# Building steps between a spectrum's products, other places for the first spectra, and nine kept blocks of weights loaded at once

## The chip, the cores and the metric

The kernel runs on one core of a Trainium2 chip. Its time is the device time of one execution in microseconds (us); lower is better. A core has TensorE (PE, matrix products into PSUM), VectorE (DVE), ScalarE (ACT), GpSimd (POOL) and SyncE (SP, which issues most of the DMAs). Each of them takes its instructions in program order, so the order in which the program emits work is the order in which each engine does it.

## What is computed

Two independent layers get the same length of sequence, 2048 rows, and their outputs stand side by side.

```
def _A_ref(x, mem0, Wq, Wk, Wv, Wo, seg_len):      # 64 segments of 32 rows, 8 memory rows
    for s in range(n_seg):
        h = concat([mem, xs])                      # q, k, v = h Wq, h Wk, h Wv; 32 heads of 128
        o = softmax(mask(q k^T)) v Wo
        mem = o[:, :M]
def _B_ref(u, A_re, A_im, B_re, B_im, C_re, C_im, log_dt, Dskip):
    K = einsum('dn,dnl,dn->dl', Cc, exp(logdA l), dB).real     # 1024 channels, 2048 taps
    y = irfft(rfft(pad(u)) * rfft(pad(K)))[:L] + u * Dskip     # a long convolution per channel
```

Layer A is a chain over 64 segments. Layer B is a convolution by Fourier transforms, which the kernel does as matrix products with tables of cosines and sines.

## The kernel before, in words

The program runs part B first (`part_b`) and then part A (`part_a`). What of part A doesn't depend on its chain is done inside part B, as side work.

Part B has these stages:

- Up to about 376 us it prepares parameters, makes tables of powers in sixteen steps (`for f in range(16)`), from which come the taps K, and beside that it transforms the input u. The transformed u goes to DRAM as `Ud`, the taps as `Kx` (copied out of a tile `KxT`, `put_values`) and, in other orders, as `Kp`.
- **The change lies from here on.** The forward matrices, which transform K, are built by `build(kc, ...)` for kc = 0 to 3: a generator of 14 steps. One step fills one PSUM bank on PE (two products of 256 columns that contract over 7 rows, L1187, or one of 512, L1191 and L1199) and empties it on ACT, with a sine (L1178) or, for the three amplitudes, a copy (L1200). Step 0 makes a basis, steps 1 to 5 the angles of half n = 0, steps 6 to 8 the amplitudes, steps 9 to 13 the angles of half n = 1. `make(kc, n)` runs the next n steps of one matrix. The banks come from a ring of three (`take`), which the tap products `kp` (`values`, L1064) use too, so a step waits until the bank used three turns before has been emptied. `weighted(kc, n)` multiplies the finished half by the amplitudes on DVE (L1209).
- `spectrum(b, n, outs)` is the product of half n of matrix b % 4 with the taps of quarter b // 4 of the channels: 20 products of 128x128 by 256 columns on PE (L1225), into two PSUM banks. Two pairs of such banks are in use (`halves`, from `ps_e`).
- The sixteen blocks `for b in range(16)` follow. `pointwise(b, s_)` multiplies the block's two spectra with u (`times_u`, two operations of L1381 per half), turns the parts (`rotate`, L1384 and L1385), and takes difference and sum (`odd` at L1471, `even` at L1472); POOL adds and subtracts those into the tile `Bt` (L1474, L1476, L1477). While it does this, the program emits the spectra of block b + 1. Each `times_u` needs its half of u, which `load_u(b)` (L1216, two loads of 512 KB into `uq`, named `wq` in the profile) fetches as soon as block b - 1 has been multiplied. From block 4 on, `inverses` does the inverse products of block b - 4 (L1513).
- `PLACES` says which of twelve slots holds which sum or difference of a quarter. Eight slots are in the tile `Bp`, which lies where `KxT` lay before; four (e2, o1, o3, s2) are in `Bq`, which lies where the tables lay. The profile calls both `Bt`.
- SP's queue in these blocks holds, in order of emission: `load_u(b + 1)`; small rearranged pieces of taps (`second`, `load_k`); pairs of skip rows (`load_pair`); two loads of 512 KB into `MI` for b < 4 (L1573), which are the inverse matrices; and then `next(resident)` as often as a table by b says: each loads 512 KB of part A's weights (L268), to be kept in SBUF. The first nine of these have memory of their own, the later ones take over places that part B has given up. Thirty have been issued after block 15 (table: 1 each for blocks 1 to 5, then 2, 2, 2, 3, 2, 3, 3, 2, 3, 3).
- Before the loop comes a hand-written order for the last table's operations (`absolute`, `minus`, `imaginary`, `cosine`, `real`, `values` and, for the copy into `KxT` at L1072, `table_ops["x"]`), matrices 0 and 1, and the spectra of blocks 0 and 1; matrix 2 is built at its end (`make(2, 14)`), matrix 3 in block 1, seven steps after each spectrum (`make(3, 7)`).

Part A then runs its 64 segments to the end, streaming a part of its weights from DRAM.

Of the kernel before, what the change touches and what calls it, by code (L numbers as in the profile page):

```python
# [687 lines left out]

COARSE = [(16, 32, 16), (544, 64, 8), (1088, 128, 8)]
FINE = [(-64, 8, 4), (-32, 4, 4), (-16, 1, 32), (16, 4, 4), (32, 8, 5)]  # L690
PLACES = ("e0 o0 e1 o1 e2 o2 e3 o3", "s0 s1 s2 s3 e0 e1 e2 e3", "o0 o1 o2 o3 s0 s2 e0 e2", "s1 s3 e1 e3 o0 o2 s0 e0")
TURNS = [(0, 1, 17), (20, 4, 4), (40, 8, 4)]
NC, NP, NN, NA = 32, 25, 24, 25
STEP, CENTER, ONE = 16, 192.0, 120
# [18 lines left out]
def part_b(ctx, tc, u, A_re, A_im, B_re, B_im, C_re, C_im, log_dt, Dskip, out_b, ahead, copies, residents, first_state):  # L713
# [6 lines left out]
    v, sc, gp, pe, sy = nc.vector, nc.scalar, nc.gpsimd, nc.tensor, nc.sync  # L720
# [57 lines left out]
    with tc.tile_pool(name="b_par", bufs=1) as par, tc.tile_pool(name="b_parh", bufs=2) as parh, \  # L778
# [190 lines left out]
        for word_ in PAR:  # L969
            word = word_.rstrip("/")  # L970
            nm, n_ = word[0], word[1:]
# [187 lines left out]
    G = {}  # L1159
# [46 lines left out]
    def weighted(kc, n_, amp):  # L1206
        a_ = amp.rearrange("p (j q) -> p j q", j=3)[:, :, 256 * n_:256 * n_ + 256]
        g_ = G[kc][:, n_, 2:5].rearrange("p j s h f -> p j s (h f)")
        v.tensor_tensor(out=g_, in0=g_, in1=a_.unsqueeze(2).to_broadcast([128, 3, 2, 256]), op=ALU.mult)  # L1209
# [5 lines left out]
        for n_ in range(2):  # L1215
            sy.dma_start(out=uq[n_], in_=Ud[b % 4, b // 4][:, 2 * n_:2 * n_ + 2].rearrange("p a c d -> p (a c d)"))  # L1216

    def spectrum(b, n_, outs, halves=(0, 1)):
        dq, kc = b // 4, b % 4
        KT = ks[dq // 2]  # L1220
        d = slice(DQ * (dq % 2), DQ * (dq % 2) + DQ)
        for half in halves:
            for cs in range(2):
                for j in range(5):
                    pe.matmul(outs[half][:, cs, :], lhsT=G[kc][:, n_, j, cs, half, :], rhs=KT[j][:, d], start=(j == 0), stop=(j == 4), skip_group_check=True)  # L1225

    T = {}
    pars = {0: par_t[0]}
# [13 lines left out]
    def cosines(r, h):  # L1242
        return T["n", r, h][:].bitcast(BF16)[:, 0:32 * NT]
# [39 lines left out]
    def cosine(r, h):  # L1283
        sc.activation(out=cosines(r, h), in_=T["n", r, h][:], func=ACT.Sin, scale=-TWO_PI, bias=hp[:])
# [5 lines left out]
    def imaginary(r, h):  # L1290
        products(r, h, "gi", windows(T.pop(("s", r, h))), T.pop(("w", r, h))[:])

    def real(r, h):
        c_ = cosines(r, h).rearrange("p (a b) -> p a b", a=32)
        products(r, h, "gr", c_, turned(c_))
# [30 lines left out]
    for f in range(16):  # L1326
# [7 lines left out]
        if f == 15:  # L1334
# [6 lines left out]
            amps = [wsl[0][:, 0:1536], wsl[3][:, 0:1536]] * 2  # L1341
# [28 lines left out]
    def make(kc, n):  # L1370
        for _ in range(n):
            next(made[kc])

    def halves(pool=ps_e):
        t_ = pool.tile([128, 2, 512], F32, name="pa", tag="pa")
        return [t_[:].rearrange("p h (c d) -> p h c d", c=2)]

    def times_u(s_, Z, n_, X=None):
        us = uq[n_].rearrange("p (a c d) -> p a c d", a=2, c=2)
        for i, t_ in ((1, Z), (0, s_[n_][0] if X is None else X)):  # L1380
            v.tensor_tensor(out=t_, in0=us[:, :, i, :].unsqueeze(2).to_broadcast([128, 2, 2, DQ]), in1=s_[n_][0], op=ALU.mult)  # L1381

    def rotate(Y, X, Z):
        v.tensor_tensor(out=Y[:, :, 0, :], in0=X[:, :, 0, :], in1=Z[:, :, 1, :], op=ALU.subtract)  # L1384
        v.tensor_tensor(out=Y[:, :, 1, :], in0=X[:, :, 1, :], in1=Z[:, :, 0, :], op=ALU.add)  # L1385
    now = [halves() for _ in range(2)]
# [2 lines left out]
    absolute(15, 0)  # L1389
    minus(15, 0)  # L1390
    make(0, 9)
    imaginary(15, 0)
    absolute(15, 1)
    minus(15, 1)
    imaginary(15, 1)
    make(0, 3)
    weighted(0, 0, amps[0])
    spectrum(0, 0, [now[0][0][:, half] for half in range(2)])
    make(0, 2)
    weighted(0, 1, amps[0])  # L1400
    spectrum(0, 1, [now[1][0][:, half] for half in range(2)])
    cosine(15, 0)
    cosine(15, 1)
    times_u(now, zs[0][:], 0, first[:, 0])
    real(15, 0)
    times_u(now, zs[1][:], 1, first[:, 1])
    load_u(1)
    real(15, 1)
    make(1, 9)
    for t in range(2):  # L1410
        values(15, t)
    make(1, 5)
    nxt_ = [halves()]
    weighted(1, 0, amps[1])
    spectrum(1, 0, [nxt_[0][0][:, half] for half in range(2)])
    for n_ in range(2):
        rotate(first[:, n_], first[:, n_], zs[n_][:])
    for t in range(2):
        table_ops["x"](15, t)
    weighted(1, 1, amps[1])  # L1420
    nxt_.append(halves())
    spectrum(1, 1, [nxt_[1][0][:, half] for half in range(2)])
    make(2, 14)
    for f_ in late:
        f_()
    for g in (pro, bg, mb, others):
# [27 lines left out]
    def spectra(dq, kc, odd_):  # L1454
        at = PLACES[dq].split()[2 * kc + odd_]
        return Bp[:, stay_.index(at)] if at in stay_ else Bq[:, ("e2", "o1", "o3", "s2").index(at)]

    def pointwise(b, s_):
        dq, kc = b // 4, b % 4
        if b:  # L1460
            times_u(s_, Zs[:, 0], 0)
            if b < 4:
                rotate(even, s_[0][0], Zs[:, 0])
            times_u(s_, Zs[:, 1], 1)
            if b > 3:
                rotate(even, s_[0][0], Zs[:, 0])
        yield
        if b:
            rotate(s_[1][0], s_[1][0], Zs[:, 1])
        Y = (even[:], s_[1][0]) if b else (first[:, 0], first[:, 1])  # L1470
        v.tensor_tensor(out=odd[:], in0=Y[0], in1=Y[1], op=ALU.subtract)  # L1471
        v.tensor_tensor(out=even[:], in0=Y[0], in1=Y[1], op=ALU.add)  # L1472
        for i, op in ((0, ALU.add), (1, ALU.subtract)):
            gp.tensor_tensor(out=spectra(dq, kc, 0)[:, i], in0=even[:, 0], in1=even[:, 1], op=op)  # L1474
        eng, to = v if b == 15 else gp, blocks(spectra(dq, kc, 1))
        eng.tensor_tensor(out=to[:, 0:4:3], in0=odd[:, 0], in1=odd[:, 1, ::-1], op=ALU.add)  # L1476
        eng.tensor_tensor(out=to[:, 2:0:-1], in0=odd[:, 0], in1=odd[:, 1, ::-1], op=ALU.subtract)  # L1477
# [52 lines left out]
    for b in range(16):  # L1530
        points = pointwise(b, now)
        next(points)
        if 0 < b < 15:
            load_u(b + 1)
        for _ in range(4 if b in (2, 3) else 0):
            second.pop(0)()
        if b == 2:
            ks.append([])
        if 2 <= b < 6:
            lo, hi = b - 2, min(b - 1, 3) if b < 5 else 5  # L1540
            ks[1].extend(load_k(1, k1[:, DH * lo:DH * hi], lo))
        if b >= 4:
            load_pair(b - 2, iv)
        if b == 3:
            v.tensor_scalar(out=ident[:], in0=ident[:], scalar1=float(PLEN / 2), scalar2=None, op0=ALU.mult)
            load_pair(0, iv)
            load_pair(1, iv)
            state = first_state(g0[0:8, 5120:6144], iv.tile([128, 8, 24], BF16, name="xt0", bufs=1))
            next(state)
            ctx_k.close()  # L1550
            ps_h = ctx.enter_context(tc.tile_pool(name="b_psh", bufs=1, space=PSUM))
            ps_y = ctx.enter_context(tc.tile_pool(name="b_psy", bufs=2, space=PSUM))
        if b == 0:
            now = nxt_
        elif b + 1 < 16:
            now = []
            for n_ in range(2):
                if b < 3:
                    if n_:
                        next(points, None)  # L1560
                    weighted(b + 1, n_, amps[b + 1])
                now.append(halves(ps_h if b > 2 and (2 * b + n_) % 3 == 0 else ps_e))
                spectrum(b + 1, n_, [now[n_][0][:, half] for half in range(2)])
                if b == 1:
                    make(3, 7)
                if b >= 4:
                    inverses(b - 4, n_)
        next(points, None)
        for n_ in (0, 1) if b == 3 else (b - 2,) if 3 < b < 15 else ():
            skips(n_, gp)  # L1570
        if b < 4:
            for i in (2 * b, 2 * b + 1):
                sy.dma_start(out=MI[i][:], in_=MId[2 * i:2 * i + 2].rearrange("c p a k q -> p c a k q"))  # L1573
        if b == 2:
            rows4 = g0[0:4, 5120:6144]
            for half in range(2):
                sy.dma_start(out=rows4[:, DH * half:DH * half + DH], in_=Kx[half][31, NF - 1].rearrange("g c -> (g c)").partition_broadcast(4))
            sy.dma_start(out=w4, in_=u[0:4, :])
            gp.tensor_tensor(out=w4, in0=rows4[:, 0:D], in1=w4, op=ALU.mult)
            gp.memset(l4, 0.0)  # L1580
            gp.memset(l4[:, :, 127:128], float(PLEN / 2))
            gp.affine_select(out=l4[:, :, 127:128], in_=l4[:, :, 127:128], compare_op=ALU.is_ge, fill=0.0, base=0, pattern=[[1, 4], [0, 1]],
                             channel_multiplier=-1)
        for _ in range({1: 1, 2: 1, 3: 1, 4: 1, 5: 1, 6: 2, 7: 2, 8: 2, 9: 3, 10: 2, 11: 3, 12: 3, 13: 2, 14: 3, 15: 3}.get(b, 0)):
            next(resident)
        if b == 10:
            state.send(ps_y.tile([128, 8, 128], BF16, name="yp", tag="yp")[:, :, 0:8])
# [180 lines left out]
```

## Time and profile before

| what | value |
|---|---|
| three runs | 1924.68, 1940.69, 1933.27 us |
| median | 1933.27 us |
| profiled execution, its own time | 1925.86 us |
| its span, first to last instruction | 1924.1 us |
| mean granted clock of TensorE in it | 0.975 |
| PE, DVE, ACT, POOL busy | 92%, 70%, 48%, 26% of the span |

Times in the profile count from the first instruction. A row of a timeline gives start, duration, engine, line, operation, what is written and read, and the shapes, and in brackets the engine's idle time before it and who ended it. A group of PE rows (x20) lasts from its first start to its last end. Durations contain a tail in which the next instruction already runs; what an instruction costs in a row of its like is the distance between starts. A row of busy time by stretch gives, for each engine, the busy time and the number of instructions, and at its end the granted clock, the mean share of the 16 DMA engines that was busy, and GB/s. A row of the waits gives the waiting engine and line, what it waited for, the total in us, how often, and the longest.

### The profile page before, as it was taken

Reading aid. Unit: us, or ns where it says so; the run is one execution under the profiler, and the core shown is the slowest. Engines: PE = TensorE matmul, PEld = TensorE weight load, DVE = VectorE, ACT = ScalarE, POOL = GpSimd, SP = SyncE. Lnnn points to the kernel's source line nnn. Section 1 sums busy time; section 2 is a strip of 40 time slices with the busy share of each in tenths; the row PEclk is TensorE's granted clock in tenths of the full one; section 3 lists DMA queues with packets and bytes.
Section 4 is the critical chain, followed back from the end, with each engine's and each line's share of the span. In section 5 each row is a group of like instructions: output and inputs, shape, how many; then the busy total and the mean of one; then the engine's idle time right before and its main releaser. Section 6 shows DMA issues by size and latency. Waiting matters only on the chain.

```text
span 1924.1 us, 73734 instructions
## 1 busy us (share of the span) xinstructions
PE 1779.6 (92%) x31563; PEld 1091.4 (57%) x31563; DVE 1346.2 (70%) x3367; ACT 919.5 (48%) x1655; POOL 508.2 (26%) x898
## 2 busy tenths in 40 slices
PE   8999999888986999999999999999999999999999
PEld 3666665546763555555555555555555555555554
DVE  8599989869992666666666666666666676666650
ACT  8799989941112444434344444444343444344330
POOL 2354544326771111111111111111111111111120
PEclk8999999868998999999999999999999999999999
DMA  7889898868899999999999999999999999999993
GB/s 223 242 237 271 242 281 239 238 171 241 287 297 367 345 328 353 348 336 352 340 347 341 339 342 350 342 343 352 340 343 333 350 355 333 341 346 344 336 336 102
DMA packets 341744, 594.21 MB, mean 309 GB/s; under 512 B 94100, under 2 KB 216476, under 8 KB 339368
## 3 DMA queue, kind: packets, MB, share of 16 engines
q1 hardware_dynamic: 297944, 534.99, 81.8%
q10 hardware_dynamic: 36816, 29.59, 4.8%
q0 software_dynamic: 6656, 24.92, 3.5%
q8 instruction: 247, 4.05, 0.8%
q14 instruction: 81, 0.66, 0.1%
HBM read 531.92 MB, written 71.63 MB: 314 GB/s over the span
## 4 chain that ended last, share of the span: by engine, by line
PE 45%; DMA 32%; DVE 14%; ACT 4%; issue 3%; POOL 2%; SPq 1%; DVEq 0%; POOLq 0%; ACTq 0%
PE acc L414 21%; DMA wst<-WD_v 12%; PE pp L527 8%; DMA wst<-WD_o 8%; DMA wst<-WD_k 3%; PE pe L667 3%; DMA arena<-PKd 2%; DMA wst<-WD_q 2%; PE tr L425 2%; DVE nr L1270 2%; PE pro L184 1%; PE pro L197 1%; PE pv L495 1%; PE pa L1225 1%; DVE gr L1236 1%
## 5 line engine op out<-in xcount | busy, mean ns | idle before, releaser
L414 PEld LDWEIGHTS <-a_hT 128*32 128x32 bf16 x12351 | 329.3, 96 | 333.8 <-issue 81.9
L420 ACT CAST arena<-acc 128x512 bf16<-128x512 f32 x384 | 225.1, 586 | 396.4 <-PE acc L414 327.2
L414 PE MATMUL acc<-wst,a_hT 128*32 128x512 bf16 x2308 | 230.7, 382 | 40.5 <-DMA wst<-WD_v 31.8
L527 PEld LDWEIGHTS <-arena 128*32 128x32 bf16 x8256 | 215.5, 96 | 72.6 <-issue 49.3
L428 POOL COPY arena<-arena 128x128 bf16<-128x128 bf16 x128 | 37.4, 292 | 695.8 <-DMA arena<-PKd 334.6
L335 DVE TENSOR_SCALAR arena<-keep 128x256 int32<-128x256 int32 x508 | 174.3, 395 | 28.3 <-PE acc L414 28.2
L414 PE MATMUL acc<-XM,a_hT 128*32 128x512 bf16 x2560 | 184.1, 380 | 0.0
L414 PE MATMUL acc<-W,a_hT 128*32 128x512 bf16 x1536 | 133.5, 385 | 0.0
L197 PE MATMUL pro<-XM,wsl 128*128 128x512 bf16 x512 | 122.7, 383 | 3.4 <-DVE kst L206 2.2
L454 DVE TENSOR_REDUCE a_mx<-sc 128x4 f32<-128x160 f32 (+1 forms) x192 | 71.8, 374 | 73.3 <-PE sc L442 71.9
L527 PE MATMUL pp<-W_o,arena 128*32 128x256 bf16 x3584 | 120.7, 273 | 0.1
L544 DVE COPY arena<-tr 128x512 bf16<-128x512 bf16 x64 | 27.2, 425 | 129.2 <-PE tr L425 129.2
L458 ACT ACTIVATE sc<-sc 128x160 f32<-128x160 f32 (+1 forms) x192 | 63.9, 333 | 104.4 <-DVE sc L455 103.5
L462 DVE TENSOR_REDUCE a_mx<-sc 128x4 f32<-128x160 f32 (+1 forms) x192 | 72.7, 379 | 55.2 <-ACT sc L458 55.0
L414 PE MATMUL acc<-W_q,a_hT 128*32 128x512 bf16 x1536 | 108.1, 379 | 0.0
L489 POOL TENSOR_TENSOR arena<-arena,a_BD 128x128 bf16<-128x128 bf16 x128 | 51.0, 399 | 212.4 <-DVE arena L472 201.6
L1270 DVE TENSOR_SCALAR nr<-ptt 128x456 f32<-128x456 int16 x128 | 80.4, 628 | 31.7 <-PE ptt L1248 28.7
L1262 ACT ACTIVATE E<-pa 128x648 bf16<-128x648 f32 x128 | 87.8, 713 | 18.0 <-PE pa L1254 16.2
L513 ACT CAST arena<-pv 128x512 bf16<-128x512 f32 (+1 forms) x128 | 61.3, 479 | 61.0 <-PE pv L499 35.9
L527 PE MATMUL pp<-wst,arena 128*32 128x256 bf16 x1536 | 76.1, 274 | 15.4 <-DMA wst<-WD_o 14.0
L623 ACT CAST arena<-pp 128x128 bf16<-128x128 f32 x64 | 17.0, 266 | 152.3 <-DVE arena L623 152.3
L425 PEld LDWEIGHTS <-arena 128*128 128x128 bf16 x1024 | 57.6, 98 | 55.1 <-issue 25.3
(332 smaller groups left out, 3965.3 us busy)
## 6 DMA issues: line engine op xcount, KB each, us to landing
wst<-WD_v SPq DMA_DIRECT2D x256, 512.0 KB
wst<-WD_k SPq DMA_DIRECT2D x192, 512.0 KB
wst<-WD_o SPq DMA_DIRECT2D x192, 512.0 KB
wst<-WD_q SPq DMA_DIRECT2D x128, 512.0 KB
Ud<-ux POOLq DMA_DIRECT2D x16, 1024.0 KB, 7.8
wq<-Ud SPq DMA_DIRECT2D x32, 512.0 KB
wsl<-in_A_Wk_dram SPq DMA_DIRECT2D x16, 512.0 KB
wsl<-in_A_Wv_dram SPq DMA_DIRECT2D x16, 512.0 KB
```

The source lines that it names most:

```text
L197: nc.tensor.matmul(a[:], lhsT=w[:, kc, 128 * j:128 * j + 128], rhs=xTl[:, kc, :, :].rearrange("p s k -> p (s k)"), start=(kc == 0), stop=( ...
L335: nc.vector.tensor_scalar(out=out.bitcast(I32), in0=in_.bitcast(I32), scalar1=0, scalar2=None, op0=ALU.bitwise_or)
L414: nc.tensor.matmul(a[32 * g:32 * g + 32, o_:o_ + rhs.shape[1]], lhsT=hT[:, kc, :], rhs=rhs, start=(kc == 0), stop=(kc == KC - 1), tile_pos ...
L420: nc.scalar.copy(out=q, in_=a[:])
L425: nc.tensor.transpose(out=p[:, hl, :, :].rearrange("p a b -> p (a b)"), in_=q[:, 128 * hl:128 * hl + 128], identity=ident[:])
L454: nc.vector.tensor_reduce(out=m_, in_=x, axis=AX.X, op=ALU.max)
L458: nc.scalar.activation(out=flat(sc, i), in_=flat(sc, i), func=ACT.Exp, scale=scale)
L462: nc.vector.tensor_reduce(out=m_, in_=x, axis=AX.X, op=ALU.add)
L513: copy(out=o[:, i:i + n], in_=p[:, i:i + n, :].rearrange("p a (g q) -> p a g q", g=4))
L527: nc.tensor.matmul(po[32 * qt:32 * qt + 32, o_:o_ + rhs.shape[1]], lhsT=oT[:, h % 4, (h % 16) // 4, :], rhs=rhs, start=False, stop=(h == 3 ...
L1262: sc.activation(out=T["E", r, e // 4][:, lo:lo + 8 * NE].rearrange("p (i c) -> p i c", i=2), in_=T.pop(("p", r, e))[:, :, 0:4 * NE], func= ...
L1270: v.tensor_scalar(out=T["n", r, e // 4][:, lo:lo + 8 * NT], in0=T.pop(("t", r, e))[:, 0:8 * NT].bitcast(I16)[:, 0:16 * NT:2], scalar1=floa ...
```

## The change

Five things are moved; no arithmetic is added or removed.

- `spectrum` gets a list `woven`: the building steps in it are emitted evenly among its 20 products, instead of standing behind the spectrum as a block. The steps of matrix 1 are woven into the spectra of block 0 (after the last two of matrix 0), those of matrix 2 into the spectra of block 1, those of matrix 3 into the spectra of block 2.
- The order ahead of the loop: each `cosine` and `real` is emitted earlier, so is `weighted(1, 0)`, and `values` stands after all of matrix 1.
- In blocks 1 and 2, `weighted(b + 1, 0)` is emitted ahead of the second half's `times_u`, instead of behind `load_u`.
- In the first quarter the sums and differences of kc 0, 1 and 2 exchange slots: those of kc 0 go to e2 and o1, both in `Bq`.
- Loads of kept weights: three each after blocks 0, 1 and 2 (nine), then 1 each for blocks 3 to 8, none for 9, one for 10, and as before from 11 on. The sum after block 15 is thirty, as before.

```diff
-PLACES = ("e0 o0 e1 o1 e2 o2 e3 o3", "s0 s1 s2 s3 e0 e1 e2 e3", ...
+PLACES = ("e2 o1 e0 o3 e1 o0 e3 o2", "s0 s1 s2 s3 e0 e1 e2 e3", ...
...
-    def spectrum(b, n_, outs, halves=(0, 1)):
+    def spectrum(b, n_, outs, woven=()):
...
-        for half in halves:
-            for cs in range(2):
-                for j in range(5):
-                    pe.matmul(outs[half][:, cs, :], lhsT=G[kc][:, n_, j, cs, half, :], rhs=KT[j][:, d], ...)
+        for i in range(20):
+            half, cs, j = i // 10, i // 5 % 2, i % 5
+            pe.matmul(outs[half][:, cs, :], lhsT=G[kc][:, n_, j, cs, half, :], rhs=KT[j][:, d], ...)
+            for k in woven[i * len(woven) // 20:(i + 1) * len(woven) // 20]:
+                make(k, 1)
...
     make(0, 9)
+    cosine(15, 0)
     imaginary(15, 0)
...
     make(0, 3)
     weighted(0, 0, amps[0])
-    spectrum(0, 0, [now[0][0][:, half] for half in range(2)])
-    make(0, 2)
+    spectrum(0, 0, [now[0][0][:, half] for half in range(2)], (0, 0, 1, 1, 1))
+    real(15, 0)
     weighted(0, 1, amps[0])
-    spectrum(0, 1, [now[1][0][:, half] for half in range(2)])
-    cosine(15, 0)
     cosine(15, 1)
+    spectrum(0, 1, [now[1][0][:, half] for half in range(2)], (1,) * 7)
     times_u(now, zs[0][:], 0, first[:, 0])
-    real(15, 0)
+    real(15, 1)
     times_u(now, zs[1][:], 1, first[:, 1])
     load_u(1)
-    real(15, 1)
-    make(1, 9)
+    make(1, 4)
+    nxt_ = [halves()]
+    weighted(1, 0, amps[1])
     for t in range(2):
         values(15, t)
-    make(1, 5)
-    nxt_ = [halves()]
-    weighted(1, 0, amps[1])
-    spectrum(1, 0, [nxt_[0][0][:, half] for half in range(2)])
+    spectrum(1, 0, [nxt_[0][0][:, half] for half in range(2)], (2,) * 7)
     for n_ in range(2):
         rotate(first[:, n_], first[:, n_], zs[n_][:])
     for t in range(2):
         table_ops["x"](15, t)
     weighted(1, 1, amps[1])
     nxt_.append(halves())
-    spectrum(1, 1, [nxt_[1][0][:, half] for half in range(2)])
-    make(2, 14)
+    spectrum(1, 1, [nxt_[1][0][:, half] for half in range(2)], (2,) * 7)
...
             if b < 4:
                 rotate(even, s_[0][0], Zs[:, 0])
+                if b < 3:
+                    weighted(b + 1, 0, amps[b + 1])
             times_u(s_, Zs[:, 1], 1)
...
-                if b < 3:
-                    if n_:
-                        next(points, None)
-                    weighted(b + 1, n_, amps[b + 1])
+                if b < 3 and n_:
+                    next(points, None)
+                    weighted(b + 1, 1, amps[b + 1])
                 now.append(halves(ps_h if b > 2 and (2 * b + n_) % 3 == 0 else ps_e))
-                spectrum(b + 1, n_, [now[n_][0][:, half] for half in range(2)])
-                if b == 1:
-                    make(3, 7)
+                spectrum(b + 1, n_, [now[n_][0][:, half] for half in range(2)], (3,) * 7 if b == 1 else ())
...
-        for _ in range({1: 1, 2: 1, 3: 1, 4: 1, 5: 1, 6: 2, 7: 2, 8: 2, 9: 3, 10: 2, 11: 3, 12: 3, 13: 2, 14: 3, 15: 3}.get(b, 0)):
+        for _ in range({0: 3, 1: 3, 2: 3, 3: 1, 4: 1, 5: 1, 6: 1, 7: 1, 8: 1, 10: 1, 11: 3, 12: 3, 13: 2, 14: 3, 15: 3}.get(b, 0)):
             next(resident)
```

More of the change, by code (lines that the diff above doesn't have):

```diff
@@ L690 @@
 FINE = [(-64, 8, 4), (-32, 4, 4), (-16, 1, 32), (16, 4, 4), (32, 8, 5)]
-PLACES = ("e0 o0 e1 o1 e2 o2 e3 o3", "s0 s1 s2 s3 e0 e1 e2 e3", "o0 o1 o2 o3 s0 s2 e0 e2", "s1 s3 e1 e3 o0 o2 s0 e0")
+PLACES = ("e2 o1 e0 o3 e1 o0 e3 o2", "s0 s1 s2 s3 e0 e1 e2 e3", "o0 o1 o2 o3 s0 s2 e0 e2", "s1 s3 e1 e3 o0 o2 s0 e0")
 TURNS = [(0, 1, 17), (20, 4, 4), (40, 8, 4)]
@@ L1221, in spectrum @@
         d = slice(DQ * (dq % 2), DQ * (dq % 2) + DQ)
-        for half in halves:
-            for cs in range(2):
-                for j in range(5):
-                    pe.matmul(outs[half][:, cs, :], lhsT=G[kc][:, n_, j, cs, half, :], rhs=KT[j][:, d], start=(j == 0), stop=(j == 4), skip_group_check=True)
+        for i in range(20):
+            half, cs, j = i // 10, i // 5 % 2, i % 5
+            pe.matmul(outs[half][:, cs, :], lhsT=G[kc][:, n_, j, cs, half, :], rhs=KT[j][:, d], start=(j == 0), stop=(j == 4), skip_group_check=True)
+            for k in woven[i * len(woven) // 20:(i + 1) * len(woven) // 20]:
+                make(k, 1)
     T = {}
```

## The prediction

> **What bounds the kernel now.** I read the page first, then busy time by stretch, then what VectorE (DVE) waits for, then each engine's timeline from 376 to 463 us. The change touches nothing before 376 us and nothing in part A, so the first view is busy time over the stage that it edits and the stage behind it.
>
> ```profile
> span 1924.1 us, 73734 instructions
> ```
> ```profile
> core 0: us, PE busy (x) PEld busy (x) DVE busy (x) ACT busy (x) POOL busy (x), PEclk, DMA share, GB/s
> 376.30:462.50 86.20, 69.46 (x501) 42.73 (x501) 65.84 (x75) 35.79 (x63) 32.10 (x29) 0.72 0.70 206
> 404.00:462.50 58.50, 48.85 (x290) 32.03 (x290) 45.62 (x50) 15.94 (x32) 30.77 (x26) 0.76 0.72 219
> 462.50:562.00 99.50, 90.39 (x780) 74.55 (x779) 97.77 (x103) 12.85 (x23) 71.44 (x53) 1.00 0.91 289
> ```
>
> From 462.5 on DVE is busy 97.77 of 99.50 us: blocks 5 to 15 run at its pace, and nothing that the change does there takes work from DVE. Everything hangs on when DVE can begin block 5, which is at 462.5 now. Before that it is busy 65.84 of 86.20 us, 20.4 us idle. What it waited for:
>
> ```profile
> DVE y L1384 <- POOL Bt L1474: 5.6, 1, 5.6
> DVE g L1209 <- ACT g L1178: 4.9, 1, 4.9
> DVE z L1381 <- PE pa L1225: 2.3, 1, 2.3
> DVE z L1381 <- DMA wq<-Ud: 2.2, 1, 2.2
> DVE XM L1209 <- ACT XM L1178: 1.8, 1, 1.8
> DVE g L1209 <- ACT wq L1200: 0.9, 1, 0.9
> DVE XM L1209 <- ACT wq L1200: 0.8, 1, 0.8
> ```
>
> These are 18.5 of the 20.4 us, and about all there is to win: some 1% of the time. One per cent (19.3 us of the median) is also about what a measurement of this kernel can tell from no change.
>
> **The clock, on which the sum turns.** The change puts small products between large ones on TensorE (PE). How fast PE then runs depends on the granted clock, which changes here only at steps of 3.41 us. Busy time, asked for in such steps (the clock is third from the right):
>
> ```profile
> 381.45:384.87 3.42, 3.42 (x13) 1.26 (x11) 2.49 (x5) 3.42 (x8) 0.00 (x0) 0.50 1.04 365
> 384.87:388.28 3.41, 3.41 (x17) 2.01 (x16) 0.74 (x1) 1.20 (x3) 0.00 (x0) 0.50 0.93 207
> 388.28:391.69 3.41, 1.78 (x15) 0.99 (x14) 1.15 (x2) 2.27 (x3) 0.00 (x0) 1.00 0.83 177
> ...
> 449.72:453.13 3.41, 2.46 (x12) 1.74 (x13) 3.41 (x4) 0.00 (x0) 2.86 (x4) 0.50 0.53 147
> 453.13:456.55 3.42, 3.42 (x18) 2.36 (x17) 3.42 (x5) 0.00 (x0) 3.42 (x4) 0.50 1.05 286
> ```
> ```profile
> 383.72 1.54 PE L1187 MATMUL gf<-g,XM 7*128 7x256 bf16 x6
> 385.19 3.88 PE L1225 MATMUL pa<-XM,g 128*128 128x256 bf16 x20
> ...
> 415.48 2.50 PE L1187 MATMUL gf<-g,XM 7*128 7x256 bf16 x10
> ...
> 421.91 4.02 PE L1225 MATMUL pa<-XM 128*128 128x256 bf16 x18 [2.55 <-DVE XM L1209]
> ...
> 458.00 2.34 PE L1225 MATMUL pa<-XM 128*128 128x256 bf16 x20
> ```
>
> The products of a building step contract over 7 rows (7*128), those of a spectrum over 128. In 381.45:384.87 PE is busy all the time with 7-row products, and the next clock is still 0.50. In 384.87:388.28 it is nearly all spectrum products, and the next is 1.00. In 449.72:453.13 twelve large products leave the clock at 0.50. So 7-row products hardly count, and somewhere between 12 and 17 large products in a step of 3.41 us raise the clock.
>
> A large product costs 0.213 us at 0.50: 256 columns at half the speed of 458.00's row (2.34 for 20 with the last one's tail, 0.107 each); 421.91's row, 18 in 4.02 with its tail, agrees. A building step is two 7-row products of 256 columns, or one of 512. No row shows its price on PE at 0.50 by itself, since ScalarE (ACT) always sets its pace there. Its bounds are 0.22 (the same columns at full clock) and 0.50 (five steps in 2.50, ACT's pace). I take 0.43, two columns' worth of spectrum products at 0.50, the nearest row. A woven group is 3 products and a step, 0.64 + 0.43 = 1.07 us, and 3.41 us hold 9.6 large products: fewer than the twelve that left the clock low. PE enters the first woven spectrum at 0.50, so I expect it to stay there to the end of the weaving. A spectrum with seven steps then costs 20 x 0.213 + 7 x 0.43 = 7.3 us.
>
> The Trainium skill, "TensorE: Matmul & The Clock Gate", section "Why this matters for your kernels", says that TensorE kept continuously busy for 4 us or more gets past the gate to the full clock. By that rule the gapless woven spectra would run at 1.00, which is the first rival; the row of 381.45 speaks against it where the products have 7 rows.
>
> **Part 1: PE's path, walked.** The rows for what stands between the spectra, on ACT, PE and DVE:
>
> ```profile
> 384.53 1.54 ACT L1178 ACTIVATE g<-gf 128x512 bf16<-128x512 int16 x3
> ...
> 390.39 3.52 ACT L1284 ACTIVATE nr<-nr,hp 128x1824 bf16<-128x1824 f32 x2
> ```
> ```profile
> 399.30 0.23 PE L1064 MATMUL kp<-gr 128*32 128x49 bf16 x4
> ...
> 400.60 0.23 PE L1064 MATMUL kp<-gi 128*32 128x49 bf16 x4
> ```
> ```profile
> 390.54 0.96 DVE L1209 TENSOR_TENSOR g<-g,wq 128x1536 bf16<-128x1536 bf16 x1 [4.93 <-ACT g L1178]
> ...
> 395.46 1.22 DVE L1381 TENSOR_TENSOR us<-wq,pa 128x1024 f32<-128x1024 f32 x1 [0.16 <-issue]
> ...
> 400.19 0.96 DVE L1209 TENSOR_TENSOR XM<-XM,wq 128x1536 bf16<-128x1536 bf16 x1 [0.85 <-ACT wq L1200]
> ...
> 403.47 1.03 DVE L1072 CAST KxT<-kp 128x392 bf16<-128x392 f32 x2
> ...
> 432.60 1.22 DVE L1381 TENSOR_TENSOR z<-wq,pa 128x1024 f32<-128x1024 f32 x1 [2.27 <-PE pa L1225]
> ...
> 439.67 0.95 DVE L1209 TENSOR_TENSOR XM<-XM,wq 128x1536 bf16<-128x1536 bf16 x1
> ...
> 450.54 1.21 DVE L1381 TENSOR_TENSOR z<-wq,pa 128x1024 f32<-128x1024 f32 x1
> ...
> 462.50 1.22 DVE L1381 TENSOR_TENSOR z<-wq,pa 128x1024 f32<-128x1024 f32 x1 [2.24 <-DMA wq<-Ud]
> ```
>
> Up to 385.2 PE's order is the old one. ACT now runs a cosine (half of 3.52, less the overlap 1.65) from 384.5, ahead of three sines; the bank that the first woven step needs comes free at 386.7, where PE wants it at 386.1: a wait of 0.6.
> - Spectrum 0,0 with five steps: 4.3 + 2.15 + 0.6, from 385.2 to 392.2.
> - Spectrum 0,1 with seven: to 399.5. The wait of 4.93 is used for the moved real part, and the weighting starts at 389.1 for 390.54; but DVE's product with u for 0,1 must wait for PE's last large product at 399.1, where it starts at 395.46 now.
> - The four steps left, at ACT's 0.5, and the 128 small kp products (1.4 us from their first to their last row): to 402.9.
> - Spectrum 1,0: its second step needs the bank that the first KxT copy frees. DVE ends the product at 401.4; weighting and four rotations take 3.3 (400.19 to 403.47), the copies 1.0: bank free at 405.2, a wait of 0.7 for PE, spectrum done at 410.8, KxT complete at 405.8 (404.5 now).
> - Spectra 1,1 and 2,0 and 2,1 at 7.3 each: 418.1, 425.4, 432.7. DVE's work between two of them is 432.60 to 440.6 less the one weighting that has moved, 7.1 us, so PE stays the later one.
>
> The last large product of 2,1 ends 0.4 before its last step, at 432.25; DVE takes it up at 432.60 now, and block 3's first weighting (0.87 start to start) already lies behind DVE then. Gain there: 0.35 + 0.87 = 1.2 us. So the 5.6, 4.9, 1.8 and 0.9 us of DVE's waits mostly come back as waits for PE at half clock.
>
> **Part 2: the first spectra's places.** GpSimd's (POOL's) first write into Bt, and the copies out of KxT:
>
> ```profile
> 414.93 2.48 POOL L1474 TENSOR_TENSOR Bt<-y 128x512 bf16<-128x512 f32 x2 [36.79 <-PE gf L1199]
> ```
> ```profile
> 404.53 5.42 SPq L1083 DMA_DIRECT2D Kx<-KxT  x4
> ```
>
> The write's input was ready 5.6 us earlier. I take it that the write waits for the copies, in whose source that part of Bt lies, while the four-slot tile lies where the tables were. With the places exchanged POOL starts with DVE's sum at 409.2 and has read it by 411.7. That removes the 5.6 us wait; what is late next is spectrum 1,1 on PE, so it is no gain of its own in the walk. If the wait stayed, to 415.2, DVE's rotation would hold back spectrum 2,0's start by 1.75 us.
>
> **Part 3: nine kept blocks early.** Seven more loads of 512 KB pass the queue of SyncE (SP) before block 4, in front of the next block's u; blocks 6 to 10 carry fewer, where DVE sets the pace (0). The price of one: 289 GB/s at a share of 0.91 is 318 GB/s when busy, 1.65 us. Its bounds and the small pieces behind block 4's u:
>
> ```profile
> 442.89:446.31 3.42, 3.42 (x34) 3.07 (x32) 3.29 (x4) 0.00 (x0) 2.56 (x3) 1.00 1.02 384
> ```
> ```profile
> DMA packets 50217, 66.63 MB, mean 273 GB/s; under 512 B 17108, under 2 KB 34524, under 8 KB 50069
> ```
> ```profile
> 449.69 4.70 DMA k<-Kx
> ```
>
> So 1.4 us (384 GB/s) to 1.9 us (273 GB/s, the mean from 376 to 620). I take 1.65, between them, and 1.4 for a load of MI, whose rows do best. The stages' DMA is busy 0.72 x 58.5 = 42.1 us from 404 to block 5; with 7 x 1.65 that is 53.7, and from 405.8 without a gap it would end at 459.5. It isn't gapless. Block 3's second half of u is issued when DVE has used block 2's, at 434.5, and lands at 436.2. Behind it: small pieces (2, half of the 4.7 us above), two MI (2.8), three kept blocks (5.0), block 4's u at 447.6 and 449.3, where DVE wants it at 449.3 (450.54 less 1.2) and 451.6; small pieces (4.0), three skips of 256 KB (2.4), two MI (2.8), a kept block (1.65) and block 5's first u at 461.8. DVE would want that at 459.1 (462.50 less its wait of 2.24, less 1.2), so this wait stays and grows to 2.7. Block 5 starts 0.7 us earlier than now, and all behind it is shifted by that: loads from block 11 on are the same, so the tail and part A are too.
>
> **Sum.** The profiled execution took 1925.86 us (its span 1924.1): 1925.2 after the change. The median of the three runs, 1933.27, is 7.4 above it: 1932.6.
>
> **The rivals.**
> - Full clock in the weaving. A woven spectrum then takes ACT's 7 x 0.5 = 3.5 us, KxT is complete at about 402, and 53.7 us of DMA end at 455.7 at the earliest, so 6 us are gained, bounded by DMA and no longer by PE: 1927.3. For it: 3.5 us at 1.00 hold 20 large products, enough to hold the clock once it is up. Against it: the rows of 381.45 and 449.72.
> - The kept blocks make u late, which ends slower. At 1.9 us a load (MI too, skips 2.9) the same chain brings block 5's u at 466.5: 4 us lost, 1937.3. It decides as soon as that u lands after 462.5, so from about 1.7 us a load. For it: the mean of 273 GB/s. Against it: 384 GB/s where the queue is full.
> - The places change nothing, and Bt's wait stays: 1.75 us worse than the forecast, 1934.3. For it: the releaser that the trace names is PE, not the copies.
>
> **How the numbers follow.** The forecast has a chance of 0.5, full clock 0.2, late u 0.2, unchanged wait 0.1. The three runs lie from 8.6 below to 7.4 above their median. The range goes from full clock's 1927.3 less 9 to late u's 1937.3 and 6: 1918 to 1943. No case moves the time by 19.3 us, so same has 0.88; faster 0.05 and slower 0.07 are for a cause that I haven't seen.
>
> **What would show it.** Right: a clock of 0.50 in each step from 378 to 432, woven spectra of some 7.3 us, no DVE wait for Bt, DVE waiting for PE's pa several times, and still for wq before block 5, near 462. Wrong: 1.00 in the weaving, block 5 begun before 459 or after 464, or a wait for wq before block 4.

## The result and the profile after

The changed kernel takes 1937.15 us (median of 22 runs, 1925.54 to 1947.33) against 1929.15 us before (22 runs, 1918.62 to 1940.69). The ratio is 1.0049, with a 95% interval from 1.0034 to 1.0065: 0.5% slower, a small loss, but a real one (the medians alone give 1.0041). Forecast was 0.7 us of gain; it lost about 8. Of the executions behind the ratios below, one of the kernel without weaving took 4306.99 us and is left out. The profiled execution took 1943.47 us, at a mean granted clock of 0.967 (before: 0.975).

First the views that answer to those of the prediction: the span; busy time over the stage and over 35 us in its middle; and what DVE waited for from 376 to 480 us.

```profile
span 1941.8 us, 73731 instructions
```
```profile
core 0: us, PE busy (x) PEld busy (x) DVE busy (x) ACT busy (x) POOL busy (x), PEclk, DMA share, GB/s
376.30:462.50 86.20, 76.68 (x500) 32.87 (x489) 60.28 (x69) 39.06 (x63) 25.14 (x26) 0.60 0.72 217
411.00:446.00 35.00, 35.00 (x132) 11.86 (x131) 21.94 (x23) 14.84 (x25) 10.52 (x8) 0.50 0.80 250
```
```profile
DVE z L1382 <- PE pa L1224: 12.5, 4, 4.1
DVE z L1382 <- DMA wq<-Ud: 5.4, 2, 4.1
DVE us L1382 <- issue: 4.4, 1, 4.4
DVE us L1382 <- PE pa L1224: 2.4, 1, 2.4
DVE g L1209 <- ACT g L1178: 1.6, 1, 1.6
```

The wait for `Bt` (5.6) is gone, and of that for ACT's sines (4.9) 1.6 is left. In their place DVE waits 12.5 us for the spectra, 5.4 for u, and 4.4 and 2.4 for the products of block 0 (`us`). The 4.4 is put down to "issue", with no releaser, since PE ran the second spectrum up to that point (its last two products end at 402.23, DVE starts at 402.32). From 411 to 446 us PE is busy in every microsecond, and its granted clock is 0.50. Now the rows of DVE that anchor all that follows, behind the sine on ACT from which I count:

```profile
379.17 1.72 ACT L1276 ACTIVATE sn<-nr 128x1824 bf16<-128x1824 f32 x1
```
```profile
423.57 1.22 DVE L1382 TENSOR_TENSOR z<-wq,pa 128x1024 f32<-128x1024 f32 x1 [4.11 <-PE pa L1224]
432.35 1.22 DVE L1382 TENSOR_TENSOR z<-wq,pa 128x1024 f32<-128x1024 f32 x1 [1.50 <-PE pa L1224]
441.14 1.22 DVE L1382 TENSOR_TENSOR z<-wq,pa 128x1024 f32<-128x1024 f32 x1 [4.11 <-PE pa L1224]
...
459.70 1.22 DVE L1382 TENSOR_TENSOR z<-wq,pa 128x1024 f32<-128x1024 f32 x1 [1.29 <-DMA wq<-Ud]
473.55 1.22 DVE L1382 TENSOR_TENSOR z<-wq,pa 128x1024 f32<-128x1024 f32 x1 [4.12 <-DMA wq<-Ud]
```

The row of 473.55 is block 5's first product. It stood at 462.50 before, so DVE begins block 5 11 us later. Block 2's second half, the row of 441.14, comes 8.9 us later than the 432.25 of the forecast (432.60 in the kernel before). Three rows in a row are 8.8 us apart: that is what a woven spectrum takes, where the forecast has 7.3.

Profiles of different kernels differ by up to 3.7 us in when part B gets here at all. So I count block 5's first product from the start of the second sine (`sn<-nr`, 379.17 above; in the profile before it stands at 378.62) and call that block 5's distance: 83.9 us before, 94.4 after, 10.5 more. The stretch ahead of that sine isn't constant either (it stands 22.0 to 23.1 us behind the second sine of the table step before, in the ten kernels without the zeros of experiment 4), so a difference of 1 us in a distance means little. The first matrix product of part A's chain comes 10.9 us later than before (597.11 for 586.16), and the first one behind part A's wait for its weights 11.7 (612.00 for 600.32), so the loss is carried into part A.

### The profile page after: what moved, and what is told of

It reads as the page before. It is cut to its first block, busy times and chain, and to the rows that moved or that the text cites. A ratio compares the mean times of both kernels' runs of the same rounds, so it can differ in the third digit from the quotient of the medians.

```text
span 1941.8 us, 73731 instructions
## 1 busy us (share of the span) xinstructions
PE 1798.2 (93%) x31563; PEld 1085.6 (56%) x31563; DVE 1346.4 (69%) x3367; ACT 922.0 (47%) x1655; POOL 509.4 (26%) x898
## 4 chain that ended last, share of the span: by engine, by line
PE 44%; DMA 34%; DVE 12%; ACT 5%; issue 3%; POOL 2%; SPq 0%; DVEq 0%; POOLq 0%; ACTq 0%
PE acc L414 20%; DMA wst<-WD_v 10%; DMA wst<-WD_o 10%; PE pp L527 7%; DMA wst<-WD_q 4%; DMA wst<-WD_k 3%; PE pe L667 3%; DMA arena<-PKd 2%; PE tr L425 2%; PE pro L184 2%; DVE nr L1271 2%; PE pa L1224 2%; PE pro L197 1%; DMA wq<-Ud 1%; PE pv L495 1%
## 5 line engine op out<-in xcount | busy, mean ns | idle before, releaser
L527 PE MATMUL pp<-wst,arena 128*32 128x256 bf16 x1536 | 76.3, 274 | 19.7 <-DMA wst<-WD_o 17.6
```

What stands on the lines that cost most here:

```text
L527: nc.tensor.matmul(po[32 * qt:32 * qt + 32, o_:o_ + rhs.shape[1]], lhsT=oT[:, h % 4, (h % 16) // 4, :], rhs=rhs, start=False, stop=(h == 3 ...
```

## The experiments

My theory after reading the two traces (theory W in the expectations): weaving itself costs the time, because each group of three spectrum products and a building step takes 1.28 us of PE and not 1.07; the early kept blocks add a few us; the new places save some. The rivals: the early loads cost it (rival 2 of the prediction, theory L), the places do, or the reordering ahead of the loop. The expectations give block 5's first product on the scale of the trace after, where it is 473.5; what follows gives distances, 94.4 for the same point.

**1. Without weaving.** The same order, but the steps of `woven` stand behind each spectrum's twenty products.

```diff
-            for k in woven[i * len(woven) // 20:(i + 1) * len(woven) // 20]:
-                make(k, 1)
+        for k in woven:
+            make(k, 1)
```

> The changed kernel, but each spectrum's building steps stand behind its 20 products instead of between them; order, places and loads as changed. Theory W (the weaving costs: clock held at 0.50, and every change between 7-row and 128-row products costs PE 0.14 us more): a spectrum's products take 4 us again, DVE's waits for PE's pa fall from 14.9 us to under 5, block 5 begins at 460 (+-3) instead of 473.5, ratio to the kernel before 0.996 to 1.000. Theory L (the nine kept blocks make u late): DVE's waits for wq stay, block 5 at 472 (+-2), ratio 1.004 to 1.006.

Measured: ratio 0.9976 to the kernel before (0.9953 to 0.9998), distance 80.8. Thus the weaving alone costs 13.6 us at block 5, more than the whole loss. PE's rows of this kernel, two spectra in one piece each, and its clock in the stage:

```profile
405.64 2.36 PE L1224 MATMUL pa<-XM 128*128 128x256 bf16 x20
...
410.77 3.84 PE L1224 MATMUL pa<-XM 128*128 128x256 bf16 x20
```
```profile
392.00:430.00 38.00, 34.33 (x301) 20.14 (x300) 31.14 (x36) 19.62 (x40) 10.53 (x8) 0.72 0.78 251
```

Some spectra get the full clock and take 2.36 us, as before the change.

**2. The old table of kept blocks.** Nine early loads undone, all else as after.

```diff
-{0: 3, 1: 3, 2: 3, 3: 1, 4: 1, 5: 1, 6: 1, 7: 1, 8: 1, 10: 1, 11: 3, ...
+{1: 1, 2: 1, 3: 1, 4: 1, 5: 1, 6: 2, 7: 2, 8: 2, 9: 3, 10: 2, 11: 3, ...
```

> The changed kernel with the table of kept blocks of the kernel before. Theory W: woven spectra stay at 8.8 us and the DVE waits for pa at 14.9; only the waits for wq shrink, from 5.4 to 2.5 us or less; block 5 at 470.5 (+-1.5), ratio 1.003 to 1.004. Theory L: block 5 back at 463, ratio 1.000.

Measured: ratio 1.0041 (1.0023 to 1.006), distance 91.1. The early loads cost 3.3 us at block 5; DVE's wait for u falls from 5.4 to 2.1, and its wait for PE stays:

```profile
DVE z L1382 <- PE pa L1224: 12.5, 4, 4.1
DVE z L1382 <- DMA wq<-Ud: 2.1, 1, 2.1
```

**3. The old places.** `PLACES` undone, all else as after.

```diff
-PLACES = ("e2 o1 e0 o3 e1 o0 e3 o2", ...
+PLACES = ("e0 o0 e1 o1 e2 o2 e3 o3", ...
```

> The changed kernel with the old slots for the first quarter's sums and differences. Theory W: GpSimd's first write waits for the copies out of KxT until about 418.3 instead of starting at 412.3, DVE's first turn of even begins at 420.8 instead of 417.3, but PE is later still (423.6), so block 5 stays at 473.5 (+-0.7), ratio 1.004 to 1.006. If the new places themselves cost something, block 5 begins earlier than in the changed kernel by more than 1 us.

Measured: ratio 1.0058 (1.0038 to 1.0078), distance 95.4. The wait for `Bt` is back, and by as much shorter is one of those for PE, so that only 1.0 us is lost. That is a little past the 0.7 expected, and no more than a distance can tell:

```profile
DVE z L1382 <- PE pa L1224: 7.5, 3, 4.0
DVE y L1385 <- POOL Bt L1474: 4.6, 1, 4.6
```

**4. The building steps' operands padded to 128 rows.** The operands of L1187, L1191 and L1199 get 121 rows of zeros, which GpSimd writes once at the start of the last table step. The values are the same, the number of products and columns too; only the 7 rows over which they contract become 128.

```diff
+            gp.memset(XT[:, 2048:3456], 0.0)
+            gp.memset(g0[:, 5120:8064], 0.0)
...
+            G.update({"rhsP": g0[:, 5120:7168], "wtsP": g0[:, 7168:7552], "basisP": g0[:, 7552:8064], "lhsP": XT[:, 2048:3456]})
...
-        rhs = G["rhs"][:, 512 * kc:512 * kc + 512]
+        rhs = G["rhsP"][:, 512 * kc:512 * kc + 512]
...
```

> The changed kernel, but the operands of the building steps are 128 rows tall, rows 7 to 127 being zeros set by GpSimd at the start of the last table step; the products are the same. Theory W: the clock rises to 1.00 within two steps of 3.4 us of the first woven spectrum and stays there; no extra time at a change of product; a spectrum with seven steps takes 3.6 to 3.9 us, ACT's pace; DVE's waits for pa under 5; block 5 at 458 (+-3), bounded by u; ratio 0.995 to 0.999. If rows only matter for the changes and not for the clock: clock 0.50, woven spectra 7.3 us, block 5 near 465. If rows matter for neither: 8.8 us and 473.

Measured: ratio 0.9973 (0.9955 to 0.9992), distance 78.2. (The zeros hold up ACT: the second sine starts at 382.42, 24.5 us behind that of the table step before, where kernels without zeros have 22.0 to 23.1. So the distance flatters this kernel by some 2 us; in its own time block 5 starts at 460.61, 12.9 before the 473.55 of after.) DVE's waits for PE's `pa` in `z` are gone; it waits 7.4 us for u instead. First PE's rows, a weight load and the clock of this kernel, then the clock in the same stretch, PE's rows and a weight load of the changed kernel:

```profile
393.49 0.38 PE L1187 MATMUL gf<-g,XM 128*128 128x256 bf16 x2
393.71 0.49 PE L1224 MATMUL pa<-XM,g 128*128 128x256 bf16 x3
394.03 0.38 PE L1187 MATMUL gf<-g,XM 128*128 128x256 bf16 x2
```
```profile
393.38 0.21 PEld L1187 LDWEIGHTS <-XM 128*128 128x128 bf16 x2
```
```profile
392.00:430.00 38.00, 24.84 (x312) 18.53 (x310) 31.02 (x34) 24.56 (x45) 10.54 (x8) 1.00 0.78 235
```
```profile
392.00:430.00 38.00, 37.52 (x262) 12.89 (x261) 24.48 (x28) 19.46 (x32) 4.93 (x4) 0.50 0.59 172
```
```profile
429.88 0.60 PE L1187 MATMUL gf<-g,XM 7*128 7x256 bf16 x2
430.42 0.82 PE L1224 MATMUL pa<-XM 128*128 128x256 bf16 x3
431.17 0.60 PE L1187 MATMUL gf<-g,XM 7*128 7x256 bf16 x2
431.70 0.61 PE L1224 MATMUL pa<-XM 128*128 128x256 bf16 x2
432.24 0.60 PE L1199 MATMUL gf<-g 7*128 7x512 bf16 x1
```
```profile
429.88 0.12 PEld L1187 LDWEIGHTS <-XM 7*128 7x128 bf16 x2 [0.41 <-issue]
```

Read the distances between starts. With 128 rows three products take 0.22 + 0.32 = 0.54 with their step, which is 5 x 0.107, and the clock is 1.00 over all the 38 us. With 7 rows, at 0.50, three large products take 0.75 from 430.42 to 431.17, where 3 x 0.213 is 0.64; the step takes 0.53, where 2 x 0.213 is 0.43. Each change between the two heights costs 0.11 us, 0.21 for a group. The weight loads show how. With 128 rows the load (393.38) starts 0.11 us ahead of its product (393.49), while the product before it runs. Behind a change (last fence) load and product start together (429.88), and PE's loads have then stood still for 0.41 us. A load takes about 0.1 us (0.21 for two), so a change costs about as much as one load that nothing hides. The Trainium skill, "TensorEngine Tiling (Array Packing)", section "Key Properties", says that a change of tiling mode drains TensorE. If a product of 7 rows runs in another mode than one of 128, this could be that drain; the records don't show the mode, the page gives no time for it, and no run here tells a drain from a load that starts late for another reason.

**5. The steps in four groups.** Two behind the 5th, 10th and 15th product each, one behind the last: eight changes of height in a spectrum with seven steps instead of fourteen.

```diff
+            if i in (4, 9, 14) or i == 19:
+                for k in woven[2 * (i // 5):2 * (i // 5) + 2]:
+                    make(k, 1)
```

> The changed kernel, but the seven steps of a spectrum stand in four groups (2, 2, 2, 1, behind products 5, 10, 15 and 20) instead of seven: as many products, six changes between 7-row and 128-row products fewer. Theory W: the clock stays 0.50 (products counted, 5 large ones and 2 steps fill 1.9 us); a spectrum with seven steps falls from 8.8 to 8.1 us (0.22 us a group less); from the second sine's start to block 5's first product 91 us (+-1) instead of 94.4. Rival (the 7-row products themselves are slower than 0.21 us at 0.50, changes cost nothing): 8.8 us, 94.4.

Measured (one execution): 1934.09 us beside 1927.55 before, distance 89.7, a spectrum 8.13 to 8.22 us instead of 8.8. The distance is just below the expected range; DVE's wait for u is 4.0 us here and not 5.4. Six changes fewer at 0.11 are 0.66: the price is per change. One group, the middle of a spectrum, where five large products cost 1.18, 0.11 above 5 x 0.213:

```profile
425.59 1.25 PE L1224 MATMUL pa<-XM 128*128 128x256 bf16 x5
426.77 0.60 PE L1199 MATMUL gf<-g 7*128 7x512 bf16 x1
427.30 1.25 PE L1224 MATMUL pa<-XM 128*128 128x256 bf16 x5
```

**6. A clock that is high when the weaving begins.** 28 more products of 128 rows in front of the first spectrum; their result is used by nothing.

```diff
+    for _ in range(28):
+        pe.matmul(now[1][0][:, 0, 0, :], lhsT=G[0][:, 0, 0, 0, 0, :], rhs=ks[0][0][:, 0:DQ], ...)
     spectrum(0, 0, [now[0][0][:, half] for half in range(2)], (0, 0, 1, 1, 1))
```

> The changed kernel with 28 extra products (128 rows, 256 columns, about 6 us at 0.50) ahead of spectrum 0,0, into a bank that spectrum 0,1 overwrites; their results are not used. Theory W with a clock that keeps its state: it is 1.00 when the weaving begins and stays there, since a woven spectrum then puts 16 or more large products into 3.4 us; such a spectrum takes 3.7 to 4.3 us, and from the second sine to block 5's first product it is 82 to 88 us, although 6 us are added. Rival (weaving pulls the clock down by itself): back to 0.50 within two steps, woven spectra 8.8 us, 100 us.

Measured (one execution): 1940.74 us beside 1927.55, distance 89.3, between the two. The rows show why it is neither:

```profile
384.42 4.77 PE L1401 MATMUL pa<-XM,g 128*128 128x256 bf16 x28
...
393.32 0.50 PE L1224 MATMUL pa<-XM,g 128*128 128x256 bf16 x3
393.75 0.39 PE L1187 MATMUL gf<-g,XM 7*128 7x256 bf16 x2
394.07 0.50 PE L1224 MATMUL pa<-XM,g 128*128 128x256 bf16 x3
```
```profile
392.00:398.50 6.50, 6.32 (x40) 2.61 (x39) 4.42 (x5) 5.94 (x10) 0.00 (x0) 1.00 0.22 79
...
402.00:439.00 37.00, 36.07 (x134) 11.16 (x133) 24.12 (x28) 16.63 (x28) 10.54 (x8) 0.50 0.79 243
```

While it is high it stays high: a woven group takes 0.75 us at 1.00 and the clock holds through both spectra of block 0. Behind them come four steps without large products and the tap products; the clock falls (0.90 in the step from 398.52), and from 402 to 439 PE is busy 36.07 of 37.00 us and doesn't get it back. And a change of height costs the same 0.11 at full clock (0.43 for 3 x 0.107, 0.32 for 2 x 0.107): it is a time and not a number of cycles of PE.

**7. Which part does what in the kernel before.** Only the new places; only the new table of kept blocks; only the 128 rows (the zeros as in 4, those for `g0` in two pieces). The two rows of waits below are of the first.

> The kernel before with the new places of the first quarter alone. Expected: GpSimd's first write starts with DVE's sum, DVE's wait of 5.6 us for Bt is gone, spectrum 2,0 starts when matrix 2 is built (3.7 us earlier); from the second sine to block 5's first product 80.2 us (+-1) instead of 83.9; ratio 0.997 to 0.9995. If the wait were not that of the copies out of KxT: wait of 5 us stays, 83.9.

> The kernel before with the new table of kept blocks alone (three after each of blocks 0, 1 and 2). Expected from the 3.3 us that the loads cost in the changed kernel: DVE waits longer for wq ahead of blocks 4 and 5; from the second sine to block 5's first product 86 us (+-1.5) instead of 83.9. If DMA has room for them here: 83.9 (+-0.5).

> The kernel before with 128-row operands for the building steps (rows 7 to 127 zeros, set by GpSimd in three pieces). Theory W: steps count as activity, the clock is 1.00 nearly throughout from 388 us on, spectra take 2.2 us instead of about 4; DVE's wait for pa goes, those for ACT and for the copies out of KxT stay; from the second sine to block 5's first product 80 to 82 us instead of 83.9; ratio 0.997 to 0.999. If the clock matters only where products are woven: 83 to 84, ratio 1.000.

Measured: the places alone 0.9986 (0.9969 to 1.0003), distance 80.3, with a wait for `Bt` of 0.4 in place of 5.6; the table alone 86.5 (one execution, 1930.04 us); the 128 rows alone 0.9997 (0.998 to 1.0014), distance 79.4. The last one misses its expectation in both. Block 5 starts 4.5 us earlier there, and the first product behind part A's wait for its weights 4.0, both counted from the second sine, and the time doesn't show it. But 4.5 us are 0.23%, only just outside the interval, and one profile each leaves chance as a possibility.

```profile
DVE y L1384 <- POOL Bt L1474: 0.4, 1, 0.4
DVE z L1381 <- DMA wq<-Ud: 0.5, 1, 0.5
```

**8. The parts put together.** The changed kernel with the old table and 128 rows; with the old table and no weaving; and with all three. The two kernels with 128 rows have the zeros for `g0` in two pieces too, and their second sine stands 22.5 us behind that of the table step before.

> The changed kernel with 128-row building steps (zeros set in three pieces, so that the first copy waits for a third of them) and the old table of kept blocks. Theory W with the loads as a second, smaller cost: DVE's waits for wq fall from 7.4 us (128 rows with nine early blocks) to under 4; from the second sine to block 5's first product 75 us (+-2); ratio 0.991 to 0.996. If the loads cost nothing once PE is fast: 78, ratio 0.997.

> The changed kernel without weaving and with the old table of kept blocks: what is left of the change is the order and the places. Theory W with loads as a second cost: DVE's waits for wq fall from 3.5 (unwoven) to 1.5 us or less; from the second sine to block 5's first product 78.5 us (+-1.5) instead of 80.8; ratio 0.994 to 0.998. If the early loads cost only where PE is late: 80.8, ratio 0.9976 as before.

> As rows128_old_loads, but without weaving: it asks what weaving itself is worth once it costs neither clock nor changes. Expected: clock 1.00 as there, spectra 2.2 us, but ACT's seven steps stand behind each spectrum again; from the second sine to block 5's first product 76 us (+-1.5), against 74.4 woven; ratio 0.993 to 0.997. If weaving is worth nothing by itself: 74.4; if DVE sets the pace with both: the same.

Measured: 0.9938 (0.9917 to 0.9959), 1914.29 us, distance 74.4; 0.9966 (0.9947 to 0.9985), distance 77.0; 0.9949 (0.9931 to 0.9967), distance 74.3. The first beats both kernels. The third misses its expectation of 76: once the rows are 128, the woven order and the plain one give the same distance, 74.4 and 74.3, and ratios that can't be told apart. So weaving shows no gain here even where it costs nothing.

All kernels that were executed more than once, in one table. The ratios are of whole executions, the distances from one profile each.

| kernel | ratio to before | block 5's distance, us |
|---|---|---|
| before | 1 | 83.9 |
| before, new places | 0.9986 | 80.3 |
| after, no weaving, old table | 0.9966 | 77.0 |
| after, no weaving | 0.9976 | 80.8 |
| after | 1.0049 | 94.4 |
| after, old table | 1.0041 | 91.1 |
| after, old places | 1.0058 | 95.4 |
| after, 128 rows | 0.9973 | 78.2 |
| after, 128 rows, old table | 0.9938 | 74.4 |
| after, 128 rows, old table, no weaving | 0.9949 | 74.3 |
| before, 128 rows | 0.9997 | 79.4 |

The first five rows go from before to after one part at a time: places -3.6, the order ahead of and in the first blocks -3.3, the early loads +3.8, the weaving +13.6, together +10.5. Taken in another order the parts change their size (the places are worth 3.6 in the kernel before and 1.0 in the one after). In the time the weaving's step is the only large one: 0.9976 to 1.0049 is 0.73% or 14 us, as at block 5. The table's step in the time is between 0.0008 and 0.0035 in the three pairs that have both; even for the largest of them, with 128 rows, the two intervals overlap (0.9955 to 0.9959).

## Why the prediction was wrong

- **The clock: right.** "I expect it to stay there to the end of the weaving": it is 0.50 in each step of 3.41 us from 381.45 to 446.31 (0.55 in the one before). The products of 7 rows do hardly count, which experiment 4 shows the other way round: the same products with 128 rows hold 1.00. By the rule of the Trainium skill that the prediction weighs ("TensorE: Matmul & The Clock Gate", section "Why this matters for your kernels": TensorE kept busy for 4 us or more reaches the full clock) the row 411.00:446.00 should be at 1.00. It is busy for 35.00 of 35.00 us at 0.50, and the measurement decides.
- **The price of a building step: this step failed.** "I take 0.43, two columns' worth of spectrum products at 0.50, the nearest row. A woven group is 3 products and a step, 0.64 + 0.43 = 1.07 us", and so "20 x 0.213 + 7 x 0.43 = 7.3 us". Measured: 1.28 us a group (430.42 to 431.70) and 8.8 a spectrum. Missing is not a share of the columns but a term of its own, two changes of height for each step at 0.11 us. 7 x 0.21 is 1.5, the whole difference. Over the five spectra with seven steps this makes 7.5 of the 8.9 us by which block 2's second half is late. The spectrum with five steps adds 1.1 and the stage's later start 0.55; shorter waits on the way take back 0.3. The step itself takes the 0.43 foreseen where its like follows it (two in 0.96 with a change, 428.48 to 429.44 in experiment 5's kernel); what was priced wrong is the sequence. With its two changes a step costs 0.64, outside the prediction's bounds of 0.22 and 0.50: these came from rows of equal products, which contain no change. And even at 7.3 us a spectrum the weaving would not have paid: the forecast amounts to a distance of 83.2 (0.7 below 83.9), and without weaving it is 80.8.
- **DVE's waits come back as waits for PE: right in kind, too small.** 12.5 and 2.4 us for PE's `pa` and the 4.4 behind the second spectrum took the place of waits that were some 13 us.
- **The places: right.** They remove the wait for `Bt` (experiment 7), so the copies out of `KxT` held it, and behind slow spectra they are worth little (1.0).
- **The early loads: the cost is right in size, its cause only half.** Forecast was a wait for u before block 5 that grows from 2.2 to 2.7, and none before block 4. Measured: 4.1 and 1.3. SP's rows of the changed kernel:

```profile
434.74 9.12 SPq L1216 DMA_DIRECT2D wq<-Ud  x2
443.91 2.73 SPq L1088 DMA_DIRECT2D Kp<-Kx  x4
...
449.46 2.43 SPq L268 DMA_DIRECT2D W_q<-in_A_Wq_dram  x3
452.78 1.94 SPq L1216 DMA_DIRECT2D wq<-Ud  x2
```
```profile
439.48:442.89 3.41, 3.41 (x16) 1.40 (x15) 1.75 (x2) 1.63 (x3) 0.00 (x0) 0.50 0.00 1
```

  SP's two loads of u take from 434.74 to 443.86, since the second has to wait until DVE has used the half before, and that waits for PE's slow spectrum; from 439.48 to 442.89 the DMA engines move nothing (share 0.00). Then the small pieces, `MI` and the three kept blocks go first, and block 4's u follows at 452.78. The prediction's chain began at 434.5; it began at 443.9. From there to block 4's u it took 15.8 us and not 13.1 (DVE starts on it at 459.70); behind that the prediction was nearly right, 13.9 us from block 4's product to block 5's (459.70 to 473.55), where it had 14.2 between the two arrivals. The early loads make this 3.3 us worse; with full clock they still cost 3.8 (78.2 against 74.4, two kernels whose zeros differ too).
- **The rivals.** Full clock as a state that the woven work can hold exists (experiment 6, with three large products every 0.75 us, where the rival had 20 in 3.5), but the kernel doesn't enter it. Late u came true in part, as a consequence of the slow spectra, and isn't the main cause: with the old table the distance is still 91.1. That its 1937.3 us lie so near the measured 1937.15 is luck. The unchanged wait is refuted.
- **The time.** 10.5 us later at block 5 agree with a ratio of 1.0049, which is 6.6 to 12.5 us. The profiled execution is 17.6 us above the one before: 11.7 of that stand at part A's first product behind the wait for its weights. The 6 behind it, which the medians don't show, need no cause of their own: from that product to the end the fourteen profiles take from 1316.6 to 1334.3 us, with the same part A. The forecast of 1932.6 us is only 4.6 below the median that came, and that is luck too: the three runs it started from have a median 4.1 above that of the 22. Of the prediction's signs of being wrong two came true: block 5 begins after 464, and there is a wait for `wq` before block 4.

**Open:** whether the 4.5 us that the kernel before gains at block 5 from the 128 rows are really missing from its time; what holds back the weight load at a change; how many rows are enough for the clock and for the changes; and whether the early loads cost in the time all that they cost at block 5.

## What to carry to other kernels

Price a sequence and not only its members: two kinds of product that are cheap in rows of their like may cost a fixed time at each change from one to the other, and weaving multiplies just the changes. Where short products must stand among tall ones, pad them with rows of zeros: here that took away the changes' cost, raised the clock and turned a loss of 0.5% into a gain of 0.3% (0.6% with the old loads). Leaving the weaving out gained 0.2% (0.3%) without any padding, and the intervals of the two overlap. And before an engine is given more even work, ask whether its neighbours' waits are on the path: with the rows padded, the times of woven and plain order can't be told apart.

## What the runs showed of the hardware

- A change between products of 7 and of 128 rows on TensorE costs 0.11 us, at a clock of 0.50 (0.75 for 3 x 0.213, 0.53 for 2 x 0.213) as at 1.00 (0.43 for 3 x 0.107, 0.32 for 2 x 0.107); the weight load behind a change starts with its product (429.88) and not 0.11 us ahead of it, as with 128 rows throughout (393.38 for 393.49).
- The granted clock goes by more than whether PE is busy. From 392 to 430 us the woven spectra ran at 0.50 with 7 rows in the steps (37.52 of 38.00 us busy) and at 1.00 with 128 (24.84 of 38.00 us busy).
- The same woven work held the clock in either state: at 1.00, where the groups came every 0.75 us, over the 9 us of two spectra (one execution, experiment 6), and at 0.50, where they came every 1.28 us, over 35 us and more.
